# Query-feature epsilon by an elementwise step instead of 32 contraction rows, with a new hand-written issue order, in a two-branch sequence-mixing kernel

## The chip, the cores and the metric

The kernel runs on one core of a Trainium2 chip. The metric is the device time of one execution, in microseconds. Three runs of the kernel before gave 160.37 us as median (159.92 to 160.57).

## The reference

Two independent branches over the same sequence length S = 2048 and width D = 576, each writing one half of the output's columns:

```python
# branch A: short shift convolution, then a long convolution by FFT, gated by q
k_shift = sum(k_pad[:, t:t + S, :] * shift_k[:, 3 - t] for t in range(4))
kv = k_shift * v
y = irfft(rfft(kv padded to 2S) * rfft(ssm_k padded to 2S))[:S]
a = q * (y + kv * ssm_D)
# branch B: linear attention with 32 heads of 18 columns
q, k, v = heads(x @ wqkv)
phi = lambda t: where(t > 0, t + 1, exp(t)) + 1e-6
pq, pk = phi(q), phi(k)
kv, z = einsum(pk, v), sum over s of pk
num, den = einsum(pq, kv), einsum(pq, z)[..., None] + 1e-6
b = (num / den) reshaped to (S, D) @ wo
return concatenate([a, b], -1)
```

## The kernel before, in words

**How the program is ordered.** The kernel records every operation in a list (`Prog.op`, line 61) with its dependencies. Nothing is scheduled at run time: the string `PLAN` (line 869) gives the whole issue order, one word per operation, its first letter the engine (P TensorE, A ScalarE, D VectorE, G GpSimd, S the DMA queue of SyncE) and the number that of the operation; `PLACES` (line 907) gives each buffer's place in SBUF or its PSUM bank. Each engine works through its own words in this order and waits where a dependency isn't met. Products of two SBUF operands are marked `two`: such a product on GpSimd waits for VectorE's last one ahead of it in the plan (lines 861 to 866).

**Branch A.** The four taps of the shift convolution are one product of 128x6144 on VectorE for each of six pieces (`conv_piece`, line 402), summed by `tap+`, in two pieces by an accumulating DMA that GpSimd issues (`acc`, line 407), and multiplied by v (`tapv`). The long convolution is a transform in two matmul stages (`s1`, line 467; `s2`, line 515) of the kernel h and of u = kv, with 32x32 transposes on VectorE between the stages (`trh`, `tru`, line 506). The product of the transforms is formed for nine column groups as `p1` and `p2` (`inv`), the latter on a copy X of the kernel's transform with its row pairs swapped. The inverse goes back through `i1` (line 551) into V and through `i2` (line 576), and the result is multiplied by q and stored (`inv2`), for three groups of 192 columns. Groups 0 and 1 go through a copy `yb`, two blocks to one product `yq`; group 2 multiplies every other block straight from PSUM (`i2q`).

**Branch B.** x is transposed, by TensorE for the first quarter (`xtr`, line 323, which needs the identity `idw`) and by DMA for the others; `kproj` (line 623) and `qproj` (line 644) are the projections, with the exponential on ScalarE and the minimum and maximum on VectorE. The reference's phi is max(t + 1, min(exp(t), 1)) + 1e-6; the kernel leaves the 1e-6 of pq out of the stored feature `pqT`. The matrix G = x^T pk (line 673) replaces a pass over v; from it come kv and z (lines 708, 722), the denominators (`den`, lines 744 and 748, with the effect of the missing 1e-6 added as `dcol`), their reciprocals (line 761), and M = kv wo (line 770). The reciprocals go to DRAM (`r_scr`) and come back spread over the rows of each head (`rb`); `pqn` multiplies pqT by them (lines 785 to 787). There are five chunks of heads (126, 126, 126, 126 and 72 rows) in each of two halves of the sequence.

**The 1e-6 of pq in the result.** Chunk 4 has only 72 of 128 rows. Rows 96 to 127 of its pqT hold the 32 reciprocals themselves (`rh`, lines 788 and 789; the rows are zeroed by `pqz`, line 280), and the same rows of M hold 1e-6 times the sum of M over the head's rows: ten matmuls with a mask (`smm`, line 798) and one VectorE operation `msev` (line 801), with rows 64 to 127 of M zeroed ahead (`Mz`, line 790). So the contraction over 128 rows in `b_out` (line 813) adds the term. `b_out` makes 16 tiles of 128 rows in two column halves, five matmuls each, copies them out of PSUM (`oev`) and stores each tile (`oo`).

**Order at the two ends.** The DMA queue starts with both halves of the first quarter of x, with the identity between them, then wk and the first rows of h. The last operations are group 0's `i2`, `yev` and `yq`, and the stores of q.

Of the kernel before, what the change touches and what calls it, by code (L numbers as in the profile page):

```python
# [13 lines left out]
S = 2048  # L14
# [10 lines left out]
HDT = []  # L25
ACC = [(0, 1), (2, 1)]
# [88 lines left out]
def _tables():  # L115
# [11 lines left out]
    E = np.empty((128, 32 + 2, 128), np.float32)  # L127
# [3 lines left out]
    W = np.zeros((32, 3, 32), np.float32)  # L131
    for bb in range(16):
        for k1 in range(16):
            p = 2.0 * np.pi * ((k1 * bb) % 16) / 16.0
            c, s = np.cos(p), np.sin(p)
            W[bb, 0, 2 * k1] = c
            W[16 + bb, 0, 2 * k1] = s
            W[bb, 0, 2 * k1 + 1] = -s
            W[16 + bb, 0, 2 * k1 + 1] = c
            W[2 * k1, 1, 2 * bb] = c  # L140
# [8 lines left out]
    for i in range(2):  # L149
        E[:, 32 + i, :] = np.kron(np.eye(4), W[:, 1 + i, :])  # L150

# [17 lines left out]
    C[:, o:o + 8] = EPS  # L169
# [14 lines left out]
def kernel(  # L184
# [49 lines left out]

    def tt(e, o, a, b, op):
# [11 lines left out]
    Esb = SB("Esb", [128, 34, 128], side=1)  # L247
# [31 lines left out]
    for f in range(2):  # L279
        P.op("G", lambda e, f=f: nc.gpsimd.memset(pqT[f].t[64:128, 4, :], 0.0), wr=[(pqT[f], (4, g)) for g in (2 * f, 2 * f + 1)] + [(pqT[f], "r")], name="pqz", ms=1024, st="pqz%d" % f)  # L280
# [4 lines left out]
    load("cst", cst, lambda e: dma(e, cst.t[:], C_d), 256 * Ct.shape[1], 1612)  # L285
    load("srow", srow, lambda e: dma(e, srow.t[:], A_shift_k.rearrange("(p d) j -> p d j", p=64)), 4608, 72, engs=EARLY)
# [4 lines left out]
    load("Esb", Esb, lambda e: dma(e, Esb.t[:].rearrange("p a c -> p (a c)"), E_d), 1114112, 8704)  # L291
# [194 lines left out]
    def s2(C, cc, pp, nm):  # L486
# [23 lines left out]
        for kh in range(4):  # L510
            ps = psb(1, "s2ps")

            def mm(e, kh=kh, ps=ps):
                for j in range(4):
                    nc.tensor.matmul(  # L515
                        ps.t[32 * j:32 * j + 32, 0, :],
                        lhsT=W2()[32 * kh:32 * kh + 32, :], rhs=ct.t[32 * kh:32 * kh + 32, 8 * j:8 * j + 8],
                        start=True, stop=True)
            P.op("P", mm, rd=[ct, idw], wr=[ps], name="s2" + nm, st=st, mm=[(512, 32, 32)] * 4)
            P.op("AD", lambda e, kh=kh, ps=ps: copy(  # L520
                e, view(sp.t[:], 32 * kh, [[256, 8], [128, 2], [1, 32]]), ps.t[:, 0, :].rearrange("p (w k t) -> p w t k", w=8, t=2)),
                 rd=[ps], wr=[(sp, kh)], name="s2ev" + nm, n=512, st=st)
# [9 lines left out]
    def inv(g, su):  # L532
# [5 lines left out]
        xb = SB("X", [128, 16, 128])  # L538
        for i in range(2):
            load("X", xb, lambda e, i=i: dma(e, xb.t[i:128:2], tx.t[1 - i:128:2]), 262144, 4096, rd=[tx], wr=[(xb, i)])  # L540
        P.op("DG", lambda e: tt(e, xb.t[:], su.t[:], xb.t[:], ALU.mult),
             rd=[su], wr=[xb], name="p2", n=2048, x2=1, two=1, st=st)
        P.op("DG", lambda e: tt(e, tx.t[:], su.t[:], tx.t[:], ALU.mult),
             rd=[su], wr=[tx], name="p1", n=2048, x2=1, two=1, st=st)
        for hh in range(4):
            ps = psb(1, "i1ps")

            def mm(e, hh=hh, ps=ps):
                for c in range(4):
                    for wi, src in ((0, tx), (1, xb)):  # L550
                        nc.tensor.matmul(ps.t[:, 0, 128 * c:128 * c + 128], lhsT=src.t[:, 4 * hh + c, :], rhs=Esb.t[:, 32 + wi, :],  # L551
                                         start=(wi == 0), stop=(wi == 1))
            P.op("P", mm, rd=[tx, xb, Esb], wr=[ps], name="i1", st=st, mm=[(128, 128, 128)] * 8)

            def ev(e, hh=hh, ps=ps):
                copy(e, view(V[gi].t[:], c0 + 4 * hh, [[n, 32], [CC // 4, 4], [1, 4]]),
                     ps.t.rearrange("p b c -> p (b c)").rearrange("p (c j r) -> p r j c", j=4, r=32))
            P.op("AD", ev, rd=[ps], wr=[(V[gi], (g, hh))], name="i1ev", n=512, st=st)
# [4 lines left out]
    def inv2(gi):  # L563
# [5 lines left out]
        for bg in range(16 // nb):  # L569
# [10 lines left out]
            if gi in YA:  # L580
# [23 lines left out]
            ns = max(nb, 4)  # L604
# [30 lines left out]
    def qproj(c, g):  # L635
        h0, hn = HCH[c]
        ps = psb(1, "qps")
        eb = SB("eq", [128, 512])
# [3 lines left out]
        def mm(e):  # L642
            for t in range(5):
                nc.tensor.matmul(ps.t[0:hn, 0, :], lhsT=wq.t[0:KT[t], t, h0:h0 + hn], rhs=xT.t[0:KT[t], t, :],  # L644
                                 start=(t == 0), stop=(t == 4))
        P.op("P", mm, rd=[xT, wq], wr=[ps], name="q", mm=[(512, 128, 126)] * 5, st=st)
        P.op("A", lambda e: nc.scalar.activation(
            out=eb.t[0:hn], in_=ps.t[0:hn, 0, :], func=ACTF.Exp, bias=neg1.t[0:hn, :]), rd=[ps, neg1], wr=[eb],
             name="qexp", n=512, st=st)
        P.op("D", lambda e: nc.vector.scalar_tensor_tensor(  # L650
            out=pqT[g // 2].t[0:hn, c, 512 * (g % 2):512 * (g % 2) + 512], in0=eb.t[0:hn],
            scalar=1.0, in1=ps.t[0:hn, 0, :], op0=ALU.min, op1=ALU.max), rd=[ps, eb], wr=[(pqT[g // 2], (c, g))], name="qphi",
             n=512, st=st)
# [3 lines left out]
    for g in range(4):  # L657
        for c in range(5):
            qproj(c, g)
# [116 lines left out]
    for f in range(2):  # L776
# [3 lines left out]
        for c, (h0, hn) in enumerate(HCH):  # L780
            rb = SB("rb", [128, 1024])
# [3 lines left out]
            P.op("DG", lambda e, c=c, hn=hn, rb=rb, f=f: tt(e, pqT[f].t[0:hn, c, :], pqT[f].t[0:hn, c, :],  # L785
                                                           rb.t[0:hn, :], ALU.mult),
                 rd=[rb], wr=[(pqT[f], (c, g)) for g in (2 * f, 2 * f + 1)], name="pqn", n=1024, x2=1, two=1)
        load("rh", None, lambda e, f=f: dma(e, pqT[f].t[96:128, 4, :], ap(r_d, 1024 * f, [[2 * S, 32], [1, 1024]])), 65536, 2048,
             rd=[(rtok, (f, 0))], wr=[(pqT[f], "r")])
    P.op("G", lambda e: nc.gpsimd.memset(M.t[64:128, 4, :], 0.0), wr=[(M, 4), (M, "s")], name="Mz", ms=576)  # L790
    for c in range(5):
        b_M(c)
    sps = psb(2, "sps")

    def smm(e):
        for hh in range(2):
            for c, (h0, hn) in enumerate(HCH):
                nc.tensor.matmul(sps.t[:, hh, 0:HALF], lhsT=hmask()[0:hn, c, :],
                                 rhs=M.t[0:hn, c, HALF * hh:HALF * hh + HALF], start=(c == 0), stop=(c == 4))
    P.op("P", smm, rd=[(M, c) for c in range(5)] + [cst], wr=[sps], name="msf", mm=[(288, 126, 128)] * 10)  # L800
    P.op("D", lambda e: nc.vector.tensor_scalar(
        out=M.t[96:128, 4, :].rearrange("p (h c) -> p h c", h=2), in0=sps.t[96:128, :, 0:HALF], scalar1=EPS, scalar2=None,
        op0=ALU.mult), rd=[sps], wr=[(M, "s")], name="msev", n=576)

    def b_out(r):
        ob = SB("ob", [128, D])
        for hh in range(2):
            ps = psb(1, "ops")

            def mm(e, hh=hh, ps=ps):  # L810
                for c, (h0, hn) in enumerate(HCH):
                    kn = 128 if c == 4 else hn
# [142 lines left out]
```

## Time and profile before

| | |
|---|---|
| median of three runs | 160.37 us (159.92 to 160.57) |
| profiled execution, first to last instruction (its span) | 158.3 us |
| TensorE busy | 149.8 us (95%) |
| VectorE busy | 141.8 us (90%) |
| ScalarE busy | 125.1 us (79%) |
| GpSimd busy | 59.6 us (38%) |
| mean granted TensorE clock | 0.994 |

The profiled execution is one run, whose own time is known only as its span, 158.3 us; the runs' times take in about 2.1 us more than it (160.37 - 158.3). In the page, part 2 cuts the span into 40 slices of 3.96 us and gives the busy share of each in tenths. A row of the groups gives line, engine, operation, output <- inputs, shapes and count, then busy time and the mean of one in ns, then idle time ahead of them. A busy matmul isn't one that streams: its start-to-start time is shorter than its length, since matmuls are pipelined. A row of the timeline gives start, length, engine, line and operation, several in a row merged with their count.

### The profile page before, as it was taken

How to read it: one execution, taken by the hardware profiler on the slowest of the kernel's cores; microseconds unless marked ns; L12 is line 12 of the kernel's file. 1: busy time of each engine (PE TensorE's matmuls, PEld its weight loads, DVE VectorE, ACT ScalarE, POOL GpSimd, SP SyncE). 2: the span in 40 equal slices, each digit the busy share in tenths (PEclk: the TensorE clock that was granted, in tenths of full speed). 3: DMA queues.
4: the chain of work that ended last, by engine and by line, in shares of the span. 5: the costliest groups of instructions: out<-in, count | busy, mean ns of one | idle time of the engine just before them, and what ended most of it. 6: DMA issues, size and time to landing. Idle time of an engine off the chain costs nothing.

```text
span 158.3 us, 4158 instructions
## 1 busy us (share of the span) xinstructions
PE 149.8 (95%) x1663; PEld 118.6 (75%) x1663; DVE 141.8 (90%) x170; ACT 125.1 (79%) x229; POOL 59.6 (38%) x53
## 2 busy tenths in 40 slices
PE   6899999999999999999999999999999999999960
PEld 2478885535679888788888887877767799999960
DVE  1547999999999998999999999999989999999690
ACT  4038999999996566467559699999899999998760
POOL 8801310011163554603611999799290000001520
PEclk9999999999999999999999999999999999999997
DMA  5999939999999809965546867881463599405766
GB/s 146 283 384 313 245 79 299 284 187 239 352 384 259 299 15 333 377 270 103 99 131 214 159 149 209 312 288 63 178 232 112 173 331 361 143 4 147 188 181 160
DMA packets 26317, 34.37 MB, mean 217 GB/s; under 512 B 15802, under 2 KB 20923, under 8 KB 25530
## 3 DMA queue, kind: packets, MB, share of 16 engines
q1 hardware_dynamic: 25754, 32.54, 66.6%
q0 software_dynamic: 544, 1.57, 5.6%
q8 instruction: 13, 0.21, 0.7%
q14 instruction: 6, 0.05, 0.1%
HBM read 20.86 MB, written 4.99 MB: 163 GB/s over the span
## 4 chain that ended last, share of the span: by engine, by line
PE 78%; ACT 8%; DVE 6%; DMA 2%; issue 1%; SPq 1%; DVEq 0%; ACTq 0%
PE ps_all L813 13%; PE ps_all L623 12%; PE ps_all L673 12%; PE ps_all L644 11%; PE ps_all L467 8%; PE ps_all L551 8%; PE ps_all L515 5%; ACT sph L229 3%; PE ps_all L576 3%; ACT V L229 3%; DMA x_sb<-in_B_x_dram 2%; PE ps_all L436 2%; DVE Ch L231 2%; ACT yb L229 1%; PE ps_all L708 1%
## 5 line engine op out<-in xcount | busy, mean ns | idle before, releaser
L644 PE MATMUL ps_all<-xT,wq 128*126 128x512 bf16 (+1 forms) x100 | 23.8, 381 | 0.1
L813 PE MATMUL ps_all<-M,pqT 126*128 126x288 bf16 (+1 forms) x160 | 22.5, 287 | 0.0
L623 PE MATMUL ps_all<-wk,xT 128*128 128x288 bf16 x160 | 20.4, 286 | 0.4 <-DVE xT L231 0.4
L402 DVE TENSOR_TENSOR m<-kh,Wj 128x6144 bf16<-128x6144 bf16 x6 | 20.1, 3349 | 0.0
L229 ACT ACTIVATE Cu<-ps_all 128x768 bf16<-128x768 f32 x22 | 17.3, 856 | 3.2 <-PE ps_all L467 3.2
L623 PEld LDWEIGHTS <-xT 128*128 128x128 bf16 x160 | 17.4, 110 | 3.1 <-DVE xT L231 0.6
L236 POOL TENSOR_TENSOR pqT<-pqT,rb 126x1024 bf16<-126x1024 bf16 (+1 forms) x9 | 19.1, 2174 | 1.0 <-DVE v L236 1.0
L813 PEld LDWEIGHTS <-pqT 126*128 126x128 bf16 (+1 forms) x160 | 16.6, 110 | 3.7 <-issue 1.9
L644 PEld LDWEIGHTS <-wq 128*126 128x126 bf16 (+1 forms) x100 | 12.5, 131 | 8.7 <-issue 2.2
L229 ACT ACTIVATE V<-ps_all 128x512 bf16<-128x512 f32 x32 | 17.2, 624 | 1.8 <-PE ps_all L551 1.8
L628 ACT ACTIVATE ek<-ps_all,neg 128x576 bf16<-128x576 f32 x16 | 11.9, 743 | 8.3 <-PE ps_all L623 8.3
L467 PEld LDWEIGHTS <-Gsb 128*128 128x128 bf16 x192 | 16.1, 98 | 2.6 <-issue 1.6
L551 PE MATMUL ps_all<-Esb,sph 128*128 128x128 bf16 x144 | 17.9, 219 | 0.1
L551 PE MATMUL ps_all<-Esb,X 128*128 128x128 bf16 x144 | 17.9, 219 | 0.0
L236 POOL TENSOR_TENSOR m<-m 128x1536 bf16<-128x1536 bf16 x4 | 12.4, 3096 | 13.1 <-DVE m L236 8.9
L673 PE MATMUL ps_all<-pk,x_sb 128*128 128x289 bf16 (+1 forms) x128 | 17.1, 287 | 0.0
L229 ACT ACTIVATE sph<-ps_all 128x512 bf16<-128x512 f32 x30 | 16.6, 608 | 0.2
L229 ACT ACTIVATE Ch<-ps_all 128x768 bf16<-128x768 f32 x19 | 15.2, 853 | 1.0 <-PE ps_all L467 0.8
L229 ACT ACTIVATE spu<-ps_all 128x512 bf16<-128x512 f32 x28 | 15.1, 613 | 0.6 <-PE ps_all L515 0.6
L236 POOL TENSOR_TENSOR q<-yb,q 128x384 bf16<-128x384 bf16 x4 | 3.6, 912 | 29.4 <-DVE yb L231 27.6
L673 PEld LDWEIGHTS <-x_sb 128*128 128x128 bf16 x128 | 12.3, 98 | 2.9
L551 PEld LDWEIGHTS <-sph 128*128 128x128 bf16 x144 | 14.0, 98 | 0.5 <-DVE sph L236 0.2
(96 smaller groups left out, 301.9 us busy)
## 6 DMA issues: line engine op xcount, KB each, us to landing
X<-sph SPq DMA_DIRECT2D x18, 256.0 KB
v<-in_A_v_dram SPq DMA_DIRECT2D x2, 1152.0 KB
out_dram<-ob SPq DMA_DIRECT2D x16, 144.0 KB
q<-in_A_q_dram SPq DMA_DIRECT2D x1, 2304.0 KB
out_dram<-q SPq DMA_DIRECT2D x12, 192.0 KB
rb<-r_scr SPq DMA_DIRECT2D x8, 252.0 KB
x_sb<-in_B_x_dram SPq DMA_DIRECT2D x3, 576.0 KB
kh<-in_A_k_dram SPq DMA_DIRECT2D x1, 1584.0 KB
```

The costliest lines, as they stand in the source:

```text
L229: nc.scalar.activation(out=o, in_=i, func=ACTF.Copy)
L236: return (nc.vector if e == "DVE" else nc.gpsimd).tensor_tensor(out=o, in0=a, in1=b, op=op)
L402: return nc.vector.tensor_tensor(out=m.t[:], in0=i0, in1=i1, op=ALU.mult)
L467: nc.tensor.matmul(ps.t[:, bank, lo - 384 * bank:hi - 384 * bank], lhsT=Gsb.t[:, b, ri, :], rhs=src[:, lo - CC * j:hi - CC * j], start=Tru ...
L515: nc.tensor.matmul(ps.t[32 * j:32 * j + 32, 0, :], lhsT=W2()[32 * kh:32 * kh + 32, :], rhs=ct.t[32 * kh:32 * kh + 32, 8 * j:8 * j + 8], st ...
L551: nc.tensor.matmul(ps.t[:, 0, 128 * c:128 * c + 128], lhsT=src.t[:, 4 * hh + c, :], rhs=Esb.t[:, 32 + wi, :], start=(wi == 0), stop=(wi == 1))
L576: nc.tensor.matmul(ps.t[:, 0, n * j:n * j + n], lhsT=Esb.t[:, 2 * b + ri, :], rhs=V[gi].t[:, 2 * b + ri, :], start=(ri == 0), stop=(ri == 1))
L623: nc.tensor.matmul(ps.t[:, hh, 0:HALF], lhsT=cols(xT.t[0:KT[t], t, :], r), rhs=wk.t[0:KT[t], t, HALF * hh:HALF * hh + HALF], start=(t == 0 ...
L628: P.op("A", lambda e: nc.scalar.activation(out=eb.t[:], in_=ps.t[:, :, 0:HALF], func=ACTF.Exp, bias=neg1.t[:]), rd=[ps, neg1], wr=[eb], na ...
L644: nc.tensor.matmul(ps.t[0:hn, 0, :], lhsT=wq.t[0:KT[t], t, h0:h0 + hn], rhs=xT.t[0:KT[t], t, :], start=(t == 0), stop=(t == 4))
L673: nc.tensor.matmul(ps.t[0:m, 0, 0:n], lhsT=x4[r // 4].t[:, r % 4, :] if t == 4 else x_sb[r // 4].t[:, r % 4, 128 * t:128 * t + 128], rhs=p ...
L813: nc.tensor.matmul(ps.t[:, 0, 0:HALF], lhsT=cols(pqT[r // 8].t[0:kn, c, 512 * (r // 4 % 2):512 * (r // 4 % 2) + 512], r), rhs=M.t[0:kn, c, ...
```

## The change

1. **Epsilon.** The ten mask matmuls `smm`, `msev`, the memsets `Mz` and `pqz`, and the loads `rh` go; the contraction of chunk 4 has 72 rows. In their place each of the ten chunk halves of pqT gets 1e-6 added in place ahead of `pqn`: `pqe`, ten operations of 126x1024 (two of them 72x1024), which the new plan puts all on GpSimd. Since `den` reads pqT without the 1e-6, they come after it.
2. **Last store in two halves.** In `inv2`, group 1's last two blocks no longer share one copy `yb` and one product: the first is multiplied straight from PSUM, the second through its own copy, and each half is stored by itself, so 13 stores of q instead of 12.
3. **Order and places.** `PLAN` and `PLACES` are new throughout. Work also changes engine: VectorE's words lose two `s1evh`, two `Mev`, two `Gev`, one `p1`, one `pqn`, one `oev` and one `hD`, and gain two `s2evh`, one `s2evu`, one `s1evu`, one `tap+`, one `tapv`, one `i2q`, one `yq` and one `x4c`; GpSimd takes both products of group 3 in `inv`. The DMA queue starts with rows of h, then both halves of x, `srow`, `wqkt`, `Drow`, and the identity as seventh. The last operations are four `i2` groups of group 0 mixed with output tiles, then `out` of two tiles, `oev` and two stores `oo`.
4. **Unused.** New branches (`ZP`, `ZA`, `MS2`, `MI1`, `MO`, `MQ`) are off. One copy of two columns (`sg`) is left, at the end of VectorE's words, and Esb has one table more (35 instead of 34).

The order of the operations on the engines around the new step, by the new plan: VectorE, after the two matmul groups `den`, has `dcol`, `den+`, `den+`, `rden`, then `tap+`, `tapv`, `tap`, a copy of one column, `tap+`, `tapv`, then `rden`, three `trh`, `tap+`, `tapv`. GpSimd has `acc`, seven `pqe`, `acc` (of the `tap` just named), `pqe`, `pqn`, `pqn`, `pqe`, `pqe`, and the other eight `pqn`.

```diff
-    for f in range(2):
-        P.op("G", lambda e, f=f: nc.gpsimd.memset(pqT[f].t[64:128, 4, :], 0.0), ...
...
+    P.op("AD", lambda e: copy(e, sgn.t[:], cs(802, 2)), rd=[cst], wr=[sgn], name="sg", n=2)
...
-            if gi in YA:
+            ya = gi in YA and not (gi == 1 and bg >= 6)
+            if ya:
...
-            ns = max(nb, 4)
+            ns = max(nb, 4) if ya or gi not in YA else nb
...
         for c, (h0, hn) in enumerate(HCH):
+            P.op("DG", lambda e, c=c, hn=hn, f=f: (nc.vector if e == "DVE" else nc.gpsimd).tensor_scalar(
+                out=pqT[f].t[0:hn, c, :], in0=pqT[f].t[0:hn, c, :], scalar1=EPS, scalar2=None, op0=ALU.add),
+                 wr=[(pqT[f], (c, g)) for g in (2 * f, 2 * f + 1)], name="pqe", n=1024)
             rb = SB("rb", [128, 1024])
...
-        load("rh", None, lambda e, f=f: dma(e, pqT[f].t[96:128, 4, :], ap(r_d, 1024 * f, [[2 * S, 32], [1, 1024]])), 65536, 2048,
-             rd=[(rtok, (f, 0))], wr=[(pqT[f], "r")])
-    P.op("G", lambda e: nc.gpsimd.memset(M.t[64:128, 4, :], 0.0), wr=[(M, 4), (M, "s")], name="Mz", ms=576)
...
-    sps = psb(2, "sps")
-
-    def smm(e):
-        for hh in range(2):
-            for c, (h0, hn) in enumerate(HCH):
-                nc.tensor.matmul(sps.t[:, hh, 0:HALF], lhsT=hmask()[0:hn, c, :],
-                                 rhs=M.t[0:hn, c, HALF * hh:HALF * hh + HALF], start=(c == 0), stop=(c == 4))
-    P.op("P", smm, rd=[(M, c) for c in range(5)] + [cst], wr=[sps], name="msf", mm=[(288, 126, 128)] * 10)
-    P.op("D", lambda e: nc.vector.tensor_scalar(
-        out=M.t[96:128, 4, :].rearrange("p (h c) -> p h c", h=2), in0=sps.t[96:128, :, 0:HALF], scalar1=EPS, scalar2=None,
-        op0=ALU.mult), rd=[sps], wr=[(M, "s")], name="msev", n=576)
...
-                    kn = 128 if c == 4 else hn
...
 PLAN = """
-G0 G6 D830 P831 G10 S28 A15 S16 G222 S26 G12 G14 G5 P30 D27 G57 P32 D33 A29 G9 G7 D31 S54 P36 A37 S53 G1 G2 S21 P34
+D835 P836 S369 S27 G1 G0 G6 G2 S25 G5 S17 D28 S53 G10 S20 S14 G26 P31 P29 A32 D30 P373 P33 D34 S52 P91 G3 S363 S50
...
 PLACES = """
...
```

More of the change, by code (lines that the diff above doesn't have):

```diff
@@ new lines, in inv @@
+        if z:
+            load("X", tx, lambda e: dma(e, tx.t[1:128:2], tx.t[0:128:2]), 262144, 4096, wr=[tx])
+        xs = su
+        if z and not za:
+            xs = SB("xs", [128, 16, 128])
+            for i in range(2):
+                load("xs", xs, lambda e, i=i: dma(e, xs.t[i:128:2], su.t[1 - i:128:2]), 262144, 4096, rd=[su], wr=[(xs, i)])
+        if z:
+            P.op("GDA", lambda e: scale(e, xb.t[:], xb.t[:], sgn.t[:, int(za):int(za) + 1]), rd=[sgn], wr=[xb], name="sgn", n=2048, st=st)
```

218 lines of the change are left out of this document (124 added, 94 removed), and 32 rows, old and new, of the table PLACES.

## The prediction

> **What bounds the kernel now.** I read the page first: the span, the busy shares and the slices.
>
> ```profile
> span 158.3 us, 4158 instructions
> PE 149.8 (95%) x1663; PEld 118.6 (75%) x1663; DVE 141.8 (90%) x170; ACT 125.1 (79%) x229; POOL 59.6 (38%) x53
> DVE  1547999999999998999999999999989999999690
> ```
>
> TensorE looks like the bound, but VectorE's row holds nines nearly without a break from the fifth slice on. So I asked for the busy time by stage. Each row has TensorE, its weight loads, VectorE, ScalarE and GpSimd in this order.
>
> ```profile
> 20.00:40.00 20.00, 19.94 (x204) 11.57 (x202) 19.91 (x20) 19.84 (x36) 1.90 (x4) 1.00 0.97 214
> 40.00:70.00 30.00, 30.00 (x223) 24.33 (x222) 29.59 (x33) 20.84 (x35) 13.06 (x6) 1.00 0.85 294
> 70.00:100.00 30.00, 29.73 (x350) 24.49 (x349) 29.57 (x33) 23.79 (x39) 17.73 (x9) 1.00 0.63 157
> 100.00:140.00 40.00, 39.92 (x559) 32.79 (x557) 38.68 (x48) 38.31 (x83) 14.61 (x6) 1.00 0.58 209
> 140.00:154.00 14.00, 13.09 (x187) 12.77 (x184) 11.95 (x22) 11.40 (x25) 3.56 (x4) 1.00 0.52 140
> ```
>
> From 20 to 140 us VectorE works 19.91 + 29.59 + 29.57 + 38.68 = 117.75 of 120 us. Two engines share the bound, and a microsecond saved on one of them alone is not a microsecond of time. GpSimd has most of its time free, and whatever goes there looks free too. Last, the tail in the timeline:
>
> ```profile
> 149.96 3.13 PE L576 MATMUL ps_all<-V,Esb 128*128 128x192 bf16 x36
> 151.89 3.23 SPq L222 DMA_DIRECT2D out_dram<-q  x5
> 153.57 1.03 DVE L236 TENSOR_TENSOR q<-yb,q 128x768 bf16<-128x768 bf16 x2
> ```
>
> The last matmul ends at 153.09, VectorE's last product at 154.60 and the last store's issue at 155.12; the span ends at 158.3, 3.2 us after that issue. VectorE is the last engine to finish.
>
> **The change part by part.** First the matmuls that go, and what VectorE loses (first the removed operation, then those that change engine) and gains.
>
> ```profile
> L798 PE MATMUL ps_all<-M,cst 126*128 126x288 bf16 x8 | 1.3, 284 | 0.0
> L801 DVE TENSOR_SCALAR M<-ps_all 32x576 bf16<-32x576 f32 x1 | 0.8, 767 | 0.0
> L231 DVE CAST Ch<-ps_all 128x768 bf16<-128x768 f32 x5 | 4.6, 962 | 0.7 <-ACT Ch L229 0.7
> L231 DVE CAST M<-ps_all 126x576 bf16<-126x576 f32 x3 | 2.3, 758 | 0.1
> L686 DVE TENSOR_SCALAR GT<-ps_all,gcol 128x288 bf16<-128x288 f32 x2 | 0.9, 475 | 0.0
> L236 DVE TENSOR_TENSOR sph<-spu,sph 128x2048 bf16<-128x2048 bf16 x9 | 10.8, 1215 | 0.0
> L236 DVE TENSOR_TENSOR pqT<-pqT,rb 126x1024 bf16<-126x1024 bf16 x1 | 0.7, 684 | 0.0
> L231 DVE CAST ob<-ps_all 128x288 bf16<-128x288 f32 x10 | 4.5, 447 | 1.3 <-PE ps_all L813 1.1
> ...
> L231 DVE CAST sph<-ps_all 128x512 bf16<-128x512 f32 x6 | 4.0, 670 | 0.0
> L231 DVE CAST Cu<-ps_all 128x768 bf16<-128x768 f32 x2 | 1.9, 932 | 0.0
> L231 DVE CAST spu<-ps_all 128x512 bf16<-128x512 f32 x8 | 5.2, 685 | 1.0 <-PE ps_all L515 1.0
> L236 DVE TENSOR_TENSOR m<-m 128x1536 bf16<-128x1536 bf16 x2 | 1.8, 920 | 0.0
> L236 DVE TENSOR_TENSOR v<-m,v 128x1536 bf16<-128x1536 bf16 x4 | 3.8, 950 | 0.0
> L236 DVE TENSOR_TENSOR q<-yb,q 128x768 bf16<-128x768 bf16 x8 | 4.2, 556 | 0.6 <-ACT yb L229 0.3
> L236 DVE TENSOR_TENSOR q<-ps_all,q 128x384 bf16<-128x384 f32 x4 | 2.2, 550 | 0.0
> ```
>
> *TensorE.* The ten mask matmuls are 1.3 us busy; on TensorE alone that is the whole gain. Since VectorE is as full, I count the gain on VectorE and not on both.
>
> *VectorE's load.* It loses 0.77 (`msev`), 2 x 0.96, 2 x 0.76, 2 x 0.48, 1.22, 0.68 and 0.45: 7.5 us. It gains 2 x 0.67, 0.93, 0.69, 0.92, 0.95, 0.56 and 0.55: 5.9 us. Net **-1.6 us**; the one `hD` less and the one `x4c` more are small and of opposite sign.
>
> *The head.* The identity was the second DMA and becomes the seventh, behind 512 KB of h. Before, the first transposes start when identity and x are there (two rows of the timeline, and the page's row of DMA rates):
>
> ```profile
> 1.22 0.42 SPq L222 DMA_DIRECT2D idw<-tab_i  x1
> 5.45 0.99 PE L323 MATMUL ps_all<-idw,x_sb 128*128 128x128 bf16 x8
> GB/s 146 283 384 313 245 79 299 284 187 239 352 384 259 299 15 333 377 270 103 99 131 214 159 149 209 312 288 63 178 232 112 173 331 361 143 4 147 188 181 160
> ```
>
> Five issues more of 0.42 us each are 2.1 us of issuing, of which some lies beside the transfers. The page's slices (the row above, each 3.96 us) show the DMA moving 0.28 to 0.38 MB a microsecond early on, so 512 KB ahead of x and the identity are 1.4 to 1.8 us; against that, h is then there for work that was done later. Bounds: -0.5 (all of it made up by the earlier h) and +2.1. I take **+1.0**, in the middle, because VectorE's early work hangs on the same transposes.
>
> *The tail.* The product, copy, product of q behind the last matmul (153.09 to 154.60, 1.5 us) go behind other matmuls: the last are now output tiles, which need one copy (0.45 us by the `ob` row) and two stores. **-1.1** for the 1.5 less 0.45; **+0.45** for a second store issued behind the first (five take 3.23, 0.65 each; the single issue at 1.22 us takes 0.42). The halved store of group 1 comes long before the end and costs nothing beside the other stores; uncovered it would be one issue, 0.65. The other loads and stores of the DMA queue change places too, the load of q among them; each still stands ahead of its first use behind work of tens of microseconds, and I count nothing for them; a transfer that comes late would show as a wait of VectorE for a DMA.
>
> *GpSimd's load.* Two memsets of 0.95 and one of M go, two products go to VectorE and one pair of `inv` comes. New are ten `pqe`. No row shows this operation on GpSimd; the nearest are these:
>
> ```profile
> L280 POOL MEMSET pqT<- 64x1024 bf16 x2 | 1.9, 947 | 0.1
> L233 POOL COPY x<-x_sb 128x256 bf16<-128x256 bf16 x1 | 0.4, 395 | 0.0
> L236 POOL TENSOR_TENSOR pqT<-pqT,rb 126x1024 bf16<-126x1024 bf16 x7 | 15.0, 2172 | 1.0 <-DVE v L236 1.0
> ```
>
> It reads one operand and writes one, as the copy does: above the memset of the same length (0.95), below the product of two (2.17). I take **1.1**. As load, eleven microseconds on an engine that is idle for 98.7 are hidden.
>
> *Where they collide.* Seven of the ten stand together directly behind `den`, and VectorE's five products of SBUF tiles (`tap+`, `tapv`, `tap`, `tap+`, `tapv`) are due in the same stretch. In before, no such product runs beside one of GpSimd; the code orders them. Nothing orders `pqe`. Does an unordered pair collide? One row says that VectorE can be held up by GpSimd's work:
>
> ```profile
> 3.63 0.31 ACT L229 ACTIVATE x<-x_sb 128x128 bf16<-128x128 bf16 x1 [1.39 <-DMA x_sb<-in_B_x_dram]
> 5.40 0.57 POOL L275 MEMSET wk<- 1x576 bf16 x1
> 5.43 1.37 DVE L231 COPY x<-x_sb 128x128 bf16<-128x128 bf16 x1 [4.02 <-DMA x_sb<-in_B_x_dram]
> 6.17 0.57 POOL L274 MEMSET wq<- 64x576 bf16 x1
> ```
>
> A copy of 128x128 takes ScalarE 0.31 us and VectorE 1.37; it starts 0.03 us behind a memset of GpSimd and ends, at 6.80, 0.06 us after the run of memsets does (6.17 + 0.57). Against it:
>
> ```profile
> 33.70 3.34 DVE L402 TENSOR_TENSOR m<-kh,Wj 128x6144 bf16<-128x6144 bf16 x1
> 35.76 0.52 POOL L349 MEMSET xT<- 1x512 bf16 x1 [2.64 <-DMA xT<-in_B_x_dram]
> ```
>
> A `tap` with a memset in its midst is not lengthened. But a memset reads nothing, and `pqe` reads.
>
> The Trainium skill (SBUF — State Buffer, "Who interferes with whom") has a rule for just this: a VectorE instruction with two SBUF inputs contends with a GpSimd instruction that reads SBUF, not with one that only writes, and the later one is blocked for the whole instruction. Both pairs of rows above agree with it; a reading operation beside a product is what no row here shows. By the rule the collision below would be certain and the sum 162.6; by the `tap` row alone it would be 159.1.
>
> If they collide, the first two or three `pqe` run beside `den+` and `rden`, which aren't products of two SBUF tiles; the other four or so alternate with the five products, each holding VectorE up by one `pqe`: 4 x 1.1 = 4.4 us. If VectorE keeps its turn instead, the `pqe` are late, and behind them on GpSimd's queue stands `acc`, whose transfer takes 6.5 us:
>
> ```profile
> m<-m POOLq DMA_DIRECT2D x2, 768.0 KB, 6.5
> ```
>
> VectorE waits for it in order with `tap+`, and `kvev`, M and all output tiles queue behind that `tap+`. Either way the loss is near 4.4. VectorE's idle time from 100 to 140 us, 40 - 38.68 = 1.3, can take up some; I let it take 0.9: **+3.5**. Bounds: 0 (no collision) and 4 x 2.17 = 8.7.
>
> *Sum.* 158.3 - 1.6 + 1.0 - 1.1 + 0.45 = 157.05 without the collision, +3.5 = 160.55 with it. The runs take in 2.07 us more than the span (160.37 - 158.3): 159.1 and **162.6 us**.
>
> **The rivals.**
>
> *No collision.* Reading `pqe` beside a product costs nothing, as the memset did: 159.1, faster by 0.8%. For it: the `tap` row. Against it: the copy row. It decides as soon as a `pqe` lies within a product and both keep their lengths.
>
> *Small collision.* `pqe` and products meet only twice, since `den` comes late or early enough that most `pqe` lie beside other work, or slack hides more: 2 x 1.1 less 0.9 = +1.3 on 159.1: 160.4, no change.
>
> *GpSimd late.* If `pqe` costs as much as a product of two, ten are 21.7 us, and `pqn` comes too late for the first output tiles as well: 8.7 - 0.9 = 7.8 on 159.1, 166.9. For it nothing but the shared engine; the copy and the memset speak against it.
>
> **How the numbers follow.** Collision 0.45 (162.6, with 161.2 to 164.5 as its own range by 3 to 5 meetings and the head's bounds), GpSimd late 0.06, no collision 0.36, small collision 0.13. About 0.5% (0.8 us) is what a measurement of this kernel can tell from no change: faster is below 159.6, slower above 161.2. So faster 0.36, same 0.13, slower 0.51. Cases of both signs hold most of the chance, so the range goes from 158.4, the case without collision with a head that costs nothing, to 164.5.
>
> **What would show it.** In the profile after: VectorE's first products behind `rden` longer than 0.92, 0.95 and 3.35 us, or with gaps ahead of them while GpSimd is in `pqe`; or `pqe` longer than 1.1 where they lie beside a product. VectorE's busy and idle time by stage: 70 to 100 us would hold the loss, later stages none. The first transposes near 6.2 us instead of 5.45. The last matmul from an output tile, and under 4.8 us from it to the end. The prediction is wrong if the products keep their lengths beside `pqe`, or if TensorE shows gaps of over a microsecond elsewhere, from the new order or places, which nothing in the profile of before can show.

## The result, and the profile after

The kernel after takes **181.52 us** (median of four runs, 180.25 to 183.84), the kernel before 160.3 beside it: 1.130 times as long, 95% interval 1.125 to 1.135. The forecast was 162.6 and its range ended at 164.5. One of the four, the profiled one at 183.84 us (span 181.8), was in a slower state than the others; the ratios and all times and differences below leave such runs out, here to a median of 181.0.

The page, with the rows that stand for before in the prediction (busy time, then VectorE's, GpSimd's and the clock's slices, each 4.5 us):

```profile
span 181.8 us, 4135 instructions
PE 154.9 (85%) x1653; PEld 121.6 (67%) x1653; DVE 146.0 (80%) x169; ACT 124.9 (69%) x230; POOL 88.4 (49%) x60
...
DVE  1324993999999999998699402998999999999891
...
POOL 3101811200355166039999999999999800005200
PEclk9978978999999999999979996558999999999999
```

In VectorE's row the hole at the start is longer than before, and there are new ones at 27 to 32 us and, the largest, at 100 to 113 us. GpSimd has gone from 59.6 to 88.4 us, and it is busy without a break just around that last hole. By stage (TensorE, its weight loads, VectorE, ScalarE, GpSimd, clock, DMA share, GB/s):

```profile
20.00:40.00 20.00, 18.16 (x179) 12.35 (x177) 16.80 (x20) 17.13 (x29) 4.66 (x9) 0.91 1.08 259
...
70.00:100.00 30.00, 25.82 (x271) 20.80 (x269) 27.56 (x24) 18.56 (x32) 20.06 (x8) 0.94 0.54 162
100.00:128.00 28.00, 16.64 (x169) 13.15 (x166) 16.45 (x18) 13.74 (x22) 27.48 (x12) 0.76 0.50 136
```

From 100 to 128 us GpSimd works 27.48 of 28 us, and TensorE and VectorE little more than half of it: for this stretch GpSimd looks like the bound. The clock granted to TensorE is 0.76 there, while TensorE is idle for 11.4 of the 28 us. The new operation, and the product behind it, in the page's groups:

```profile
L821 POOL TENSOR_SCALAR pqT<-pqT 126x1024 bf16<-126x1024 bf16 (+1 forms) x10 | 31.7, 3168 | 2.6 <-PE ps_all L788 2.0
...
L253 POOL TENSOR_TENSOR pqT<-pqT,rb 126x1024 bf16<-126x1024 bf16 (+1 forms) x10 | 20.9, 2128 | 0.2
```

A `pqe` takes 3.17 us in the mean, not the 1.1 I took; it is dearer than the product of two operands (2.13). What stands behind it shows in GpSimd's timeline and in the chain that ended last:

```profile
82.08 23.18 POOL L821 TENSOR_SCALAR pqT<-pqT 126x1024 bf16<-126x1024 bf16 x7 [1.96 <-PE ps_all L788]
105.30 1.22 POOL L424 DMA_DIRECT2D m<-m  x1
106.60 2.76 POOL L821 TENSOR_SCALAR pqT<-pqT 126x1024 bf16<-126x1024 bf16 x1
109.44 4.18 POOL L253 TENSOR_TENSOR pqT<-pqT,rb 126x1024 bf16<-126x1024 bf16 x2
113.71 6.21 POOL L821 TENSOR_SCALAR pqT<-pqT 126x1024 bf16<-126x1024 bf16 x2
120.00 8.37 POOL L253 TENSOR_TENSOR pqT<-pqT,rb 126x1024 bf16<-126x1024 bf16 x4
```

```profile
17.08 7.22 DMA hs<-in_A_ssm_k_dram
...
78.74 9.31 DMA m<-m
...
102.50 2.77 POOL pqT L821
105.30 7.20 DMA m<-m
112.53 1.93 DVE m L253
```

Seven `pqe` run from 82.08 to 105.26; only then is the second accumulate issued, though its `tap` had ended at 94.1. VectorE's rows say what that costs and what the collisions cost:

```profile
89.06 1.67 DVE L253 TENSOR_TENSOR v<-m,v 128x1536 bf16<-128x1536 bf16 x1
90.77 3.36 DVE L419 TENSOR_TENSOR m<-kh,Wj 128x6144 bf16<-128x6144 bf16 x1
...
94.11 1.72 DVE L253 TENSOR_TENSOR m<-m 128x1536 bf16<-128x1536 bf16 x1
95.87 0.96 DVE L253 TENSOR_TENSOR v<-m,v 128x1536 bf16<-128x1536 bf16 x1
...
112.53 1.92 DVE L253 TENSOR_TENSOR m<-m 128x1536 bf16<-128x1536 bf16 x1 [10.68 <-DMA m<-m]
114.48 1.67 DVE L253 TENSOR_TENSOR v<-m,v 128x1536 bf16<-128x1536 bf16 x1
```

VectorE waits 10.68 us for the accumulate. Of these products of two, the four that lie beside a `pqe` or (at 112.53) mostly beside a `pqn` take 1.67, 1.72, 1.92 and 1.67 us where those alone take 0.95: 3.2 us in all. The `tap` keeps its 3.36.

### The profile page after: what moved, and what is told of

Same layout as the page of the kernel before. It is cut to its first block, busy times and chain, and to the rows that moved or that the text cites. A ratio compares the mean times of both kernels' runs of the same rounds, so it can differ in the third digit from the quotient of the medians.

```text
span 181.8 us, 4135 instructions
## 1 busy us (share of the span) xinstructions
PE 154.9 (85%) x1653; PEld 121.6 (67%) x1653; DVE 146.0 (80%) x169; ACT 124.9 (69%) x230; POOL 88.4 (49%) x60
## 4 chain that ended last, share of the span: by engine, by line
DVE 33%; PE 32%; DMA 16%; issue 6%; POOL 5%; SPq 3%; ACT 2%; DVEq 0%; POOLq 0%; ACTq 0%
PE ps_all L841 10%; DMA m<-m 9%; PE ps_all L589 9%; DVE m L419 7%; DVE pqT L690 6%; DVE m L253 5%; POOL pqT L821 5%; DVE pk L670 5%; PE ps_all L614 4%; DMA hs<-in_A_ssm_k_dram 4%; DMA wk<-in_B_wqkv_dram 3%; DVE ct L523 3%; PE ps_all L534 3%; DVE v L253 3%; SPq L233 3%
## 5 line engine op out<-in xcount | busy, mean ns | idle before, releaser
L821 POOL TENSOR_SCALAR pqT<-pqT 126x1024 bf16<-126x1024 bf16 (+1 forms) x10 | 31.7, 3168 | 2.6 <-PE ps_all L788 2.0
L484 PEld LDWEIGHTS <-Gsb 128*128 128x128 bf16 x192 | 17.9, 106 | 17.8 <-DVE v L253 11.0
L484 PE MATMUL ps_all<-v,Gsb 128*128 128x192 bf16 x96 | 11.8, 276 | 13.9 <-DVE v L253 10.4
L662 PE MATMUL ps_all<-wk,xT 128*128 128x288 bf16 x160 | 21.7, 293 | 1.9 <-DMA wk<-in_B_wqkv_dram 1.9
L841 PE MATMUL ps_all<-M,pqT 126*128 126x288 bf16 (+1 forms) x160 | 22.7, 287 | 0.0
L253 DVE TENSOR_TENSOR m<-m 128x3072 bf16<-128x3072 bf16 (+1 forms) x7 | 11.7, 1667 | 12.8 <-DMA m<-m 12.8
L253 POOL TENSOR_TENSOR pqT<-pqT,rb 126x1024 bf16<-126x1024 bf16 (+1 forms) x10 | 20.9, 2128 | 0.2
L841 PEld LDWEIGHTS <-pqT 126*128 126x128 bf16 (+1 forms) x160 | 16.5, 110 | 4.1 <-issue 2.3
L253 POOL TENSOR_TENSOR hT<-hT,Drow 1x128 bf16<-1x128 bf16 (+2 forms) x6 | 2.1, 355 | 35.1 <-DVE m L253 15.4
L240 ACT ACTIVATE Ch<-ps_all 128x768 bf16<-128x768 f32 x21 | 16.5, 846 | 2.5 <-PE ps_all L484 2.5
L240 ACT ACTIVATE sph<-ps_all 128x512 bf16<-128x512 f32 x28 | 15.5, 614 | 1.8 <-PE ps_all L534 1.6
L687 ACT ACTIVATE eq<-ps_all,neg 126x512 bf16<-126x512 f32 (+1 forms) x20 | 13.4, 693 | 4.2 <-DVE pk L670 2.8
```

The source lines that it names most:

```text
L240: nc.scalar.activation(out=o, in_=i, func=ACTF.Copy)
L253: return (nc.vector if e == "DVE" else nc.gpsimd).tensor_tensor(out=o, in0=a, in1=b, op=op)
L484: nc.tensor.matmul(ps.t[:, bank, lo - 384 * bank:hi - 384 * bank], lhsT=Gsb.t[:, b, ri, :], rhs=src[:, lo - CC * j:hi - CC * j], start=Tru ...
L662: nc.tensor.matmul(ps.t[:, hh, 0:HALF], lhsT=cols(xT.t[0:KT[t], t, :], r), rhs=wk.t[0:KT[t], t, HALF * hh:HALF * hh + HALF], start=(t == 0 ...
L687: P.op("A", lambda e: nc.scalar.activation(out=eb.t[0:hn], in_=ps.t[0:hn], func=ACTF.Exp, bias=neg1.t[0:hn, :]), rd=[ps, neg1], wr=[eb], n ...
L821: P.op("DG", lambda e, c=c, hn=hn, f=f: (nc.vector if e == "DVE" else nc.gpsimd).tensor_scalar(out=pqT[f].t[0:hn, c, :], in0=pqT[f].t[0:hn ...
```

## The experiments

Theory after this reading: the price of `pqe` on GpSimd is the loss, by way of the accumulate behind it, and the head is a term of its own. Rivals: the collisions; or the new order and places are slow by themselves. All ratios are to the kernel before on the same chip (159.9 to 160.2 us). Where a kernel is built on "thin", epsilon is left out as its expectation says.

### The price of pqe taken away, moved, and its queue changed

*Thin* adds epsilon to `pqT[f].t[0:1, c, 0:2]` alone, in the same places of the order:

```diff
-                out=pqT[f].t[0:hn, c, :], in0=pqT[f].t[0:hn, c, :], scalar1=EPS, ...
+                out=pqT[f].t[0:1, c, 0:2], in0=pqT[f].t[0:1, c, 0:2], scalar1=EPS, ...
```

> The ten pqe keep their places, waits and semaphores but each adds epsilon to one partition of two elements only (so the epsilon of the query features is left out but for these). Theory (the price of pqe on GpSimd, 2.77 us each, holds the second accumulate behind it): the accumulate goes out within 1 us of its product, VectorE's wait of 10.7 us for it falls under 4, and the time to 163 to 167 us; what is left over 160.3 is the head, about 5 us. Rival collision (only the lengthening of VectorE's products counts): 3.2 us less, about 178. Rival order (the new order and places are slow by themselves, pqe only happens to stand there): 175 or more.

Measured 172.22 us, 1.075 times before (1.072 to 1.079). The price with all that hangs on it is 181.0 - 172.2 = **8.8 us**, less than half of the 20.8 lost. The waits of VectorE in it:

```profile
DVE m L253 <- DMA m<-m: 5.6, 2, 3.3
```

The wait of 10.7 is now 3.3, as the theory has it, but 12 us stay that it does not explain. Neither the theory's 163 to 167 nor the order rival's 175 was met: both hold a part.

*On VectorE*: the ten words of `pqe` in PLAN go from G to D.

> The ten pqe are done by VectorE at the same places of the order; nothing else changes. Theory (price on GpSimd): VectorE takes 0.3 to 0.7 us for each, 3 to 7 in all, of which those ahead of the accumulate's product count least; GpSimd is free for the accumulate: 166 to 171 us. Rival collision: products no longer lengthened (3.2 less) but 3 to 7 more on VectorE: 178 to 185. Rival order: 181 or more.

1.085 times before (1.078 to 1.093), which is 173.9 us. That is 7.1 off, most of the 8.8: most of the price is GpSimd's, and not that of the add. VectorE's adds take 0.42 us in the median (0.39 to 2.34), against 2.77 on GpSimd.

*Accumulate first*: the word G84 (`acc`) goes from behind the seventh `pqe` to behind the third.

> Only the second accumulate's issue moves on GpSimd's queue: behind the third pqe instead of behind the seventh. Theory (the queue behind pqe holds the accumulate): it goes out near 95 us instead of 105.3, VectorE's wait of 10.7 us falls by 6 or more, M comes earlier by 6 to 9, and the time is 172 to 177; the pqe still to come delay pqn, so not all of it is regained. Rival collision: the products meet as many pqe as before, 181 to 183. Rival order: 181 to 183.

182.1 us, 1.134 (1.126 to 1.142): nothing gained. The accumulate goes out 12 us earlier than in the kernel after (second row), and VectorE's waits for the two accumulates fall from 12.8 us to 4.5. So the theory's queue was there, but to shorten it buys no time. GpSimd's timeline says why:

```profile
81.57 9.51 POOL L821 TENSOR_SCALAR pqT<-pqT 126x1024 bf16<-126x1024 bf16 x3 [1.96 <-PE ps_all L788]
92.87 1.22 POOL L424 DMA_DIRECT2D m<-m  x1 [1.79 <-DVE gcol L242]
94.17 14.28 POOL L821 TENSOR_SCALAR pqT<-pqT 126x1024 bf16<-126x1024 bf16 x5
...
118.52 16.71 POOL L253 TENSOR_TENSOR pqT<-pqT,rb 126x1024 bf16<-126x1024 bf16 x8
```

```profile
DVE m L253 <- DMA m<-m: 4.5, 2, 3.7
PE ps_all L841 <- POOL pqT L253: 5.8, 3, 2.5
```

GpSimd has 20 operations on pqT to do before the last output tiles, and works at them to 135.2 us whatever stands first. TensorE's output tiles (L841) now wait for `pqn` instead, 5.8 us in all. What is late is the sum of GpSimd's work, wherever the accumulate stands in it.

### The same add in the old order

The add is put ahead of each product `pqn` in the kernel before, first on the product's own engine (GpSimd for nine), then all on VectorE:

```diff
+            def pn(e, c=c, hn=hn, rb=rb, f=f):
+                (nc.vector if e == "DVE" else nc.gpsimd).tensor_scalar(out=pqT[f].t[0:hn, c, :], in0=pqT[f].t[0:hn, c, :], scalar1=EPS, ...)
+                return tt(e, pqT[f].t[0:hn, c, :], pqT[f].t[0:hn, c, :], rb.t[0:hn, :], ALU.mult)
```

> The kernel before, its order and places kept; each product pqn is preceded on its own engine (GpSimd for nine, VectorE for one) by the same add of epsilon in place as pqe. Epsilon is then in twice, by the rows and by the add. Theory (the price of pqe on GpSimd is a loss in any order, since pqn are late by it): nine adds of 2.77 are 25 us more on GpSimd between 87.6 and 110, output tiles wait for the last pqn, and the time grows by 5 to 12, to 165 to 172. Rival (it is the new order that makes pqe dear; GpSimd's idle time hides them): 160 to 162.

187.32 us, 1.173 (1.170 to 1.175): 27 us more, where the nine adds are 9 x 2.77 = 25. GpSimd's rows, add and product by turns:

```profile
87.76 2.78 POOL L786 TENSOR_SCALAR pqT<-pqT 126x1024 bf16<-126x1024 bf16 x1
90.62 2.13 POOL L236 TENSOR_TENSOR pqT<-pqT,rb 126x1024 bf16<-126x1024 bf16 x1
```

So the idle time of GpSimd hid nothing of them: an engine at 38% can be the bound in the one stage where its result is due. The loss in size is far above what I expected, in direction it is the theory's.

> As the run before, but all ten adds on VectorE, just ahead of the products, in the old order and places. Theory (0.39 us each on a VectorE that is full): 3 to 4.5 more, 163 to 165. Rival (VectorE's load is not the bound there; TensorE is): within 1 us of 160.2. A third outcome, 166 or more, would say that the waits between the engines cost more than the adds.

170.96 us, 1.070 (1.068 to 1.072), the third outcome. Beside GpSimd's products VectorE's add isn't 0.39 us:

```profile
104.12 1.55 DVE L786 TENSOR_SCALAR pqT<-pqT 126x1024 bf16<-126x1024 bf16 x1
...
106.46 2.34 DVE L786 TENSOR_SCALAR pqT<-pqT 126x1024 bf16<-126x1024 bf16 x1
...
119.15 0.39 DVE L786 TENSOR_SCALAR pqT<-pqT 126x1024 bf16<-126x1024 bf16 x1
```

and the ten together take 9.3 us of VectorE, where 0.39 each would be 3.9. GpSimd's products wait for an add five times, 2.9 us in all. So the same adds were put in one block ahead of the first `pqn`, in a kernel before without the epsilon rows, which was also run by itself:

> The kernel before, its order and places kept, with the epsilon rows of the output tiles taken out: the nine of ten mask matmuls, the scaled eviction msev, the two memsets of 0.95 us, that of M and the two loads of the extra rows are each shrunk to two elements or left out, and the output tiles contract 72 rows instead of 128 in the fifth chunk. The epsilon of the query features is left out. This is all that the change can save. Theory (TensorE 1.3, VectorE 0.8, memsets in idle time): 0.8 to 1.6 us faster, 158.4 to 159.4. Rival (M's evictions and the mask matmuls are a chain on the way to the first output tile): 3 us or more faster, 157 or less.

159.88 us, 0.998 (0.996 to 1.000). All that the change removes is worth about 0.3 us, and the interval reaches to nothing. TensorE and VectorE both lose work there; why next to nothing of it reaches the end, the run doesn't show.

> The run before this one, with the ten adds of epsilon on VectorE in one block just ahead of its own product pqn, where GpSimd has no product under way: the change itself in the old order and places. Theory (0.39 us each when no product of GpSimd lies beside it, VectorE full): 3 to 4.5 above the run without epsilon, 161.5 to 164. Rival (the adds cost VectorE what they cost in the run with the adds ahead of each product, 0.9 us in the mean, or they hold the products behind): 168 or more.

162.87 us, 1.017 (1.013 to 1.020): 3.0 above the run without epsilon, the least that was expected. The adds, apart from GpSimd's products, in the groups of that run:

```profile
L789 DVE TENSOR_SCALAR pqT<-pqT 126x1024 bf16<-126x1024 bf16 x8 | 2.9, 420 | 0.0
```

This is the epsilon step itself at its cheapest place tried, and it still costs 2.7 us against before: it saves 0.3 and spends 3.

### What makes the add dear

Four of the ten `pqe` in other forms on GpSimd:

```diff
+                if (f, c) == (1, 1): return nc.gpsimd.tensor_copy(out=x, in_=x)
+                if (f, c) == (1, 2): return nc.gpsimd.tensor_tensor(out=x, in0=x, in1=x, op=ALU.add)
+                if (f, c) == (0, 0): return nc.gpsimd.tensor_scalar(out=x, in0=x, scalar1=1.0, scalar2=None, op0=ALU.mult)
+                if (f, c) == (0, 3): x = pqT[f].t[0:hn, c, 0:512]
```

> The kernel after with four of its ten pqe in other forms on GpSimd, for their durations alone: one a copy in place, one a sum of two SBUF operands (the chunk with itself, so its features are doubled), one a multiplication by one, one the add over 512 of the 1024 elements; these leave epsilon out, the last for half its elements. If the price lies in the operation with a constant: copy 1.3 to 1.7 us, sum of two 2.13, multiplication 2.77, half the elements 1.4. Rival (in-place reading and writing of one buffer is what costs): copy and multiplication both near 2.77, and the sum of two as well.

One run, 179.42 us. From the groups and the timeline:

```profile
L828 POOL TENSOR_SCALAR pqT<-pqT 126x1024 bf16<-126x1024 bf16 x1 | 2.8, 2782 | 0.1
L826 POOL TENSOR_TENSOR pqT<-pqT 126x1024 bf16<-126x1024 bf16 x1 | 2.4, 2382 | 0.0
L831 POOL TENSOR_SCALAR pqT<-pqT 126x512 bf16<-126x512 bf16 x1 | 1.8, 1762 | 0.1
```

```profile
97.77 1.04 POOL L824 COPY pqT<-pqT 126x1024 bf16<-126x1024 bf16 x1
```

The copy in place takes 1.04 us, the operation with a constant 2.78 whether it adds or multiplies, and half the elements 1.76. So neither reading nor working in place is dear on GpSimd, but the arithmetic with a constant is. My 1.1 was the price of a copy.

### The head

The store `ww` (word S23), which waits for ScalarE's `wjt`, moves on the DMA queue from ahead of four loads to behind the fourth piece of h (S470):

> Only the small store ww moves on the load queue, from ahead of four loads to behind the fourth piece of h. Theory (in the head the queue stands still until ww's input is there): the fourth piece of h is issued near 9 to 10 us instead of 17.1, lands near 17 instead of 24.3, the start of s2h0 comes from 30.8 to 26 or 27, and the time falls by 3 to 5, to 176.5 to 178.5. Rival (VectorE or the pqe stage takes up what the head gives): the milestones of the head move and the time stays within 1 us of 181.5.

178.75 us, 1.120 (1.113 to 1.127): 2.2 less. In the kernel after the queue issues nothing between 8.71 us and `ww`:

```profile
13.84 0.69 SPq L233 DMA_DIRECT2D w_scr<-srt  x1
```

With `ww` moved the queue stands still all the same, until 12.48 us, now ahead of a load `kh`; what holds it there isn't shown. The fourth piece of h goes out at 14.70 us instead of 17.08, not at 9 to 10, and the first `s2` of h starts at 25.2 instead of 30.8. Of these 5.6 us 2.2 reach the end. With thin `pqe`:

> The thin pqe (epsilon left out of the query features but for two elements each) and the store ww behind the fourth piece of h, together. What is left over 160.2 is then neither the price of pqe nor the queue in the head. Theory (the two are separate terms): the head gives 3 to 5.5 here too, 166.5 to 169; some 6 to 9 remain for the other order and places (VectorE's two waits for accumulates, 5.6 in the thin kernel, first among them). Rival (the head's delay is taken up later by the waits of VectorE for the accumulates): within 1.5 us of 172.2.

170.04 us, 1.064 (1.058 to 1.070): 2.2 less than thin alone, under what was expected, and 10 us remain. With `pqe` on VectorE and `ww` moved:

> pqe on VectorE at 0.4 us each and ww behind the fourth piece of h. Theory (separate terms): 2 to 3 above the thin kernel with the same ww, 169 to 172. Rival (VectorE's waits hide its ten pqe): the same time as the thin kernel with ww, within 1 us.

173.36 us, 1.084 (1.078 to 1.091): 3.3 above thin, near the 3.0 of the old order but over the 169 to 172 expected. Here `ww` gives only 0.5 (from 173.9), less than the interval of that run, 1.3 each way, can tell.

Where the 10 us lie shows in VectorE's busy time by stretch, first before, then thin with `ww` moved (busy, count, clock, DMA share, GB/s):

```profile
0.00:20.00 20.00, 11.54 (x19) 1.00 0.93 276
20.00:80.00 60.00, 59.42 (x61) 1.00 0.83 235
80.00:100.00 20.00, 19.64 (x24) 1.00 0.69 186
```

```profile
0.00:20.00 20.00, 7.85 (x14) 1.00 0.92 254
20.00:80.00 60.00, 59.60 (x63) 1.00 0.68 196
80.00:100.00 20.00, 14.18 (x12) 0.91 0.62 157
```

3.7 us are lost in the first 20, nothing from 20 to 80, and 5.5 from 80 to 100: together 9.2 of the 9.6 by which the spans differ (167.9 and 158.3).

For the first part, the loads of the head were put back as before (x, identity, x and wk ahead of h: words S27 S14 S25 S53 S52 S17 S20 ahead of S369), in the thin kernel with `ww` moved and in the one with full `pqe`:

> The kernel with thin pqe and ww moved (epsilon left out but for two elements each), with the head's loads as before the change: x, identity, x and wk ahead of the first piece of h. Theory (a): the first transposes start near 5.5 instead of 8 us, VectorE's idle time in the first 20 us falls by 2.5 to 3.5, and the time by 2 to 3.5, to 166.5 to 168. Rival (c): the head's gain is taken up in the middle stage, within 1 us of 170.0.

> The kernel after with its full pqe on GpSimd, ww moved and the head's loads as before the change. Theory (the price of pqe and the head are separate terms, and the head is worth 4.5 to 6 in all): 175.5 to 177. Rival (the head's gain is lost behind pqe and the accumulate): 178 or more.

173.05 us, 1.082 (1.079 to 1.086), and 182.08, 1.139 (1.136 to 1.142): slower by 3.0 and by 3.3 than without this step. TensorE's timeline in the first of them:

```profile
6.11 1.06 PE L340 MATMUL ps_all<-idw,x_sb 128*128 128x128 bf16 x8
10.27 1.07 PE L453 MATMUL ps_all<-idw,hs 128*128 128x128 bf16 x8 [3.10 <-DMA hs<-in_A_ssm_k_dram]
11.14 1.06 PE L340 MATMUL ps_all<-idw,x_sb 128*128 128x128 bf16 x8
```

The transpositions of h stand in TensorE's queue ahead of the other half of those of x, and now wait 3.10 us for h. A queue's order and the loads' order are one thing; undoing half of it says nothing about the whole. Moving the identity alone to third place:

> The kernel with thin pqe and ww moved (epsilon left out but for two elements each), with the identity's load moved up from seventh to third place, behind the first piece of h and the first half of x; nothing else. Theory (the head hangs on the identity): the second transposes start near 6.5 instead of 7.6 us, VectorE's idle time at 20 us falls by about 1, the time by 0.7 to 1.5 from 170.0. Rival (the matmuls of h in the queue ahead, or wk, set the head): within 0.5 us.

169.4 us, 1.062 (1.055 to 1.069): no gain clear of the noise. VectorE copies the first transpositions at 7.47 instead of 8.87 us, but the first operation of branch B behind them (on `pk`) comes at 12.43, without this step at 12.80. TensorE's timeline shows what stands ahead of it:

```profile
10.08 1.39 PE L662 MATMUL ps_all<-wk,xT 128*128 128x288 bf16 x10 [1.70 <-DMA wk<-in_B_wqkv_dram]
```

The first projection now waits 1.70 us for wk. It starts at 10.08 us, at 10.33 without this step and at 8.20 in the kernel before. So the identity and wk hold the head one behind the other, and to move one alone gains next to nothing, as the rival had it; both together, with an order of TensorE to match, weren't tried.

### The middle stage

In the new order the last `tap+` is VectorE's and stands ahead of the transpositions of u; before, it was GpSimd's and VectorE waited for no accumulate at all. In the thin kernel with `ww` moved its two waits, 2.3 and 3.4 us, are nearly all of the 5.8 us that it is idle from 80 to 100. Ready work was put ahead of the two `tap+` (D235 ahead of D69; P539, A540 and D583 ahead of D85):

> The kernel with thin pqe and ww moved (epsilon left out but for two elements each), and ready work put ahead of VectorE's two waits for the accumulates: one rden ahead of the first tap+, one transposition ahead of the second. Theory (the two waits, 2.3 and 3.4 us, are a term of the time): 1.7 and 1.2 us of work go into the waits, 2 to 3 off, 167 to 168.2. Rival (TensorE or a DMA sets that stretch): within 0.8 us of 170.

170.2 us, 1.061 (1.056 to 1.066): no gain. The sum of the waits fell to 4.1 us, but the second kept 3.6. More could not be put there: PLACES gives the first transposition of u the bytes that this `tap+` reads, so moving `tap+` behind it was not tried in the new kernel. In the old one the step can be made alone (G86 becomes D86, and D86 and D87 go ahead of D558):

> The kernel before with one step changed: the last tap+ and its tapv are on VectorE ahead of the three transpositions of u, as in the kernel after, instead of on GpSimd and behind the evictions of M. Theory (the new place of tap+ puts VectorE, and kvev, M and the output tiles behind it, into a wait for the second accumulate): VectorE comes there at about 90.7 us, the accumulate lands at about 94, so a wait of 2.5 to 4 appears and the time grows by 2.5 to 5, to 162.5 to 165. Rival (the slack behind takes it up): within 1 us of 160.2.

**164.27 us**, 1.027 (1.024 to 1.030): 4.3 us for one step. VectorE's timeline:

```profile
88.69 2.36 DVE L506 STREAM_TRANSPOSE ct<-Ch 128x1024 f32<-128x1024 f32 x2
93.10 0.96 DVE L236 TENSOR_TENSOR m<-m 128x1536 bf16<-128x1536 bf16 x1 [2.05 <-DMA m<-m]
94.09 0.96 DVE L236 TENSOR_TENSOR v<-m,v 128x1536 bf16<-128x1536 bf16 x1
94.97 1.24 DVE L506 STREAM_TRANSPOSE ct<-Cu 128x1024 f32<-128x1024 f32 x1
```

The wait is 2.05 us, less than expected; the two products of 0.96 that now stand ahead of the transpositions come on top, and `kvev` and M behind them are late by both.

### Late products side by side

In the thin kernel with `ww` moved, VectorE's product `p2` of `inv5` lies beside one of GpSimd's two of `inv3` (4.07 us each) and takes 4.0 instead of 1.2. `inv3` on VectorE instead (G631 and G632 become D):

> The kernel with thin pqe and ww moved (epsilon left out but for two elements each), with p1 and p2 of inv3 on VectorE instead of GpSimd. Theory (b): p2 of inv5 takes 1.2 instead of 4.0 us, the two added products 1.2 each, so VectorE's load changes by -0.4, and the waits for GpSimd's products of 4.06 go: 1 to 2.5 off, 167.5 to 169. Rival (c): within 0.8 us of 170.0.

170.6 us, 1.062 (1.055 to 1.068): no gain, though all 18 products of VectorE then took 1.2 us. With the head's loads and the filled waits as well:

> Both of these, and the ready work put ahead of VectorE's two waits. If head and late products are separate terms of 2 to 3.5 and 1 to 2.5: 164 to 166.5, and 4 to 6 over the kernel before are left for the middle stage. Rival (c): 168.5 or more.

171.20 us, 1.070 (1.065 to 1.074): 1.2 more than without the three steps, less than the 3.0 that the head's loads alone cost. The steps don't add up, and which of them gave some back no run shows.

## Why the prediction was wrong, point by point

**The price of `pqe`.** This is the step that failed first: "It reads one operand and writes one, as the copy does: above the memset of the same length (0.95), below the product of two (2.17). I take 1.1." A copy of that size takes 1.04, so the row was read rightly; but the nearest row to an add is the one that does arithmetic. 2.77 lies above the upper bound I set. The Trainium skill (GPSIMD Engine Reference, 4.1 Engine selection) says that GpSimd does one-input operations at roughly line rate; for the add with a constant the runs disagree, 2.77 us against VectorE's 0.39 and against GpSimd's own copy of 1.04.

**"Eleven microseconds on an engine that is idle for 98.7 are hidden."** Idle over the whole span, but not between `den` and the output tiles: there `pqe` and `pqn` are one chain. The old order with the adds on GpSimd lost 27 us for 25 of work. In the new order the price is 8.8, a third of that; that other waits lie beside it there is the likely reason, and isn't shown.

**The collision.** The likeliest case was right that they meet: 3.2 us on VectorE, near the 4.4 before slack, and a `pqe` beside a product was lengthened too, from 2.77 up to 5.04. What this is worth in time no run separates from the price of `pqe`; thin takes away both. The Trainium skill's rule (SBUF — State Buffer, "Who interferes with whom" and, for the block, "SBUF: two separate sides") is borne out in that such pairs contend. That the later one is blocked for the whole instruction is not: the `tap+` at 94.11 ended at 95.83, while the `pqe` beside it, begun at 91.72, ran to 96.76. The copy row, which the prediction counted for the rule, has one input and a memset beside it, so the rule for products of two says nothing of it. Nor does the code order all such pairs: it holds GpSimd's products behind VectorE's, and not the other way. So VectorE's `p2` at 142.95 us met a product of GpSimd and took 2.92 us instead of 1.21.

**"GpSimd late", chance 0.06.** The right mechanism with too low a price (2.17) and too little hung on it. It named that `pqn` comes too late for the first output tiles; the run with the accumulate put first showed just that.

**The moved steps.** This is the second step that failed. I counted "nothing" for the other loads and stores of the DMA queue. `ww` stands ahead of the fourth piece of h (issued at 17.08 in the chain) and costs 2.2. The `tap+` that changes engine I counted as 0.92 us of load; its wait for the accumulate, ahead of the transpositions, cost 4.3 in the old order and is by VectorE's idle time the best account of the 5.5 in the new.

**The head.** +1.0 was too little; VectorE's idle time says 3.7 beyond `ww`. Some 2 of it are the start of the first projection (10.33 instead of 8.20 us), for which the identity and wk come late one behind the other; I had followed the identity alone. The rest is open: neither the loads' order nor the identity alone gave time back, and the engines' order there was not undone.

**The load of VectorE and the removed work.** With the epsilon rows gone the old kernel gains 0.3 us. I had a net -1.6 for the load, on the assumption that an engine 98% busy turns every microsecond saved into time. Nor did the load fall: VectorE is busy 146.0 us after and 142.4 with thin `pqe`, against 141.8 before.

**The tail** was right in sign, and more than twice the size. ScalarE's last copy starts when the last matmul, an output tile's, has ended:

```profile
178.18 0.41 ACT L240 ACTIVATE ob<-ps_all 128x288 bf16<-128x288 f32 x1 [0.21 <-PE ps_all L841]
```

The span ends at 181.8, 3.6 us later, against 5.2 before (153.09 to 158.3): -1.6 where I had -1.1 + 0.45.

**The signs it named.** The products were lengthened, `pqe` took more than 1.1, the first transposes began late (6.73 us, forecast 6.2), and an output tile came last. But the loss was to lie from 70 to 100 us, and later stages were to hold none; VectorE is idle 2.4 us of those 30 and 11.6 of the 28 that follow. That it would be slower had 0.51, on the collision; most of the loss has other sources, so the right direction is in good part luck.

The terms: price 8.8 (8.7 and 9.0 in the two other pairs with and without thin, 178.75 to 170.04 and 182.08 to 173.05), `ww` 2.2; of the 10.0 left, about 5.5 in the middle stage and 3.7 in the head, by VectorE's idle time. The first two are shown by runs. The last two are read from the profile: the middle one has a run in the old order alone (4.3), and no run gave either back in the new.

## What to carry to other kernels

Price a new operation by a row of the same kind (arithmetic, copy, fill) on the same engine, and not by the number of its operands; if there is no such row, let the range reach above the dearest one. An engine's idle share says nothing about the stage in which its result is due: add the new work to its chain there. A step that moves to another engine brings its waits along, and all that is queued behind it pays for them.

## What the runs showed of the hardware that I had not expected

GpSimd's operation with a constant takes 2.77 us for 126x1024 bf16, more than its sum of two operands (2.38) and its product of two (2.13), and a copy takes 1.04. It takes 2.77 for 72 partitions as well. VectorE's add with a constant takes 0.39 alone and up to 2.34 beside a product of GpSimd. TensorE's granted clock fell to 0.76 from 100 to 128 us, where TensorE was busy 16.64 of 28 us.
